# A first phase without lead pieces: reloads in another order, stores on ScalarE's queue, positions on SyncE's

## The chip, the cores and the metric

The kernel runs on one core of a Trainium2 chip. A core has five engines, each with its own instruction stream that it works through in order: TensorE (PE, matrix products), VectorE (DVE), ScalarE (ACT), GpSimd (POOL) and SyncE (SP, which computes nothing). SyncE, ScalarE and GpSimd also issue DMA transfers between the chip's memory (DRAM) and the core's on-chip memory; the core's 16 DMA engines carry them out. An instruction can wait for others by semaphores, and while it waits everything behind it on its engine waits too.

The metric is the time of one execution in device microseconds, lower is better. Most executions of one kernel agree within 0.3%.

## The reference

Two stages. The first convolves the product of x and v with a learned filter along the sequence, by Fourier transforms, and gates the result with x. The second sends about half of the rows through one of eight small expert networks. The change lies in the first stage.

```python
def _attn_ref(x, v, pos_emb, w1, w2):         # x, v: (4, 11456, 128)
    B, S, D = x.shape
    h_mlp = np.maximum(pos_emb @ w1, 0.0) @ w2     # pos_emb: (11456, 64)
    h_filt = h_mlp * np.exp(-0.01 * np.arange(S))[:, None]
    L = 2 * S
    Uf = np.fft.rfft(x * v, n=L, axis=1)
    Hf = np.fft.rfft(h_filt, n=L, axis=0)
    y = np.fft.irfft(Uf * Hf[None], n=L, axis=1)[:, :S]
    return x * y
...
    # then, row by row: if x @ w_skip > 0: out = x + gate * relu(x @ w1[e]) @ w2[e], else out = x
```

All of it is in float32.

## The kernel before

The sequence is cut into three blocks of 3840 = 60 x 64 rows, and the transform of one block is done in two steps: 60 points (k1) in a first phase, 64 points in a second, with the twiddle factors folded into the second one's matrices. The 128 channels are cut into four strips of 32. A *data step* is a sixteenth of a strip: it loads x and v (`wf<-xv`, 768 KB), multiplies them, transforms over 60 points (L202, two pieces of two products each), copies the result out of PSUM on ScalarE (L204) and stores it to DRAM (`x1d<-wf`, 720 KB). The strips have 64 steps in all, 0 to 15 for strip 0, and so on. The 64-point transform needs all steps of a strip, since it reads the stored rows in the other direction; that is why they go through DRAM.

**First phase** (`first_phase`, L276). It does the 16 data steps of strip 0 and, interleaved with them at a fixed pace, the filter (`First.filt`, L214): 12 position pieces (`post`, 256 KB each, L232, loaded from GpSimd's queue) go through w1 (L240, result `fa`) and relu (L241, `h`); then 24 groups go through w2 (L267), the window (L268, `hw`), the 60-point transform (L248) and a copy (L250, `fx`), and are stored to `x1f` in 16 transfers of 720 KB from GpSimd's queue (L256).

**Frequency phase** (`freq_phase`, L307). It runs 60 rounds, 15 for each strip. A round loads four k1 of a strip (`x<-x1d`, 768 KB, L362, and `x<-x1f`, 192 KB, L363; in strip 0 the matrix `c2` too, 256 KB, L359), three rounds ahead into four buffers; transforms them on PE (L373, `xp`); multiplies data and filter on VectorE (L385 to L393); adds on GpSimd (L465, L466); transforms back on PE (L404); copies on ScalarE (L405, `z`) and stores `zd` (L414). The data steps of the next strip are spread over the rounds of this one (`step`, L344): they must be done four rounds before the next strip begins. A round has one or two of them.

What sets the order around the change:

- Both phases are recorded in a fixed order, which is the order of the code on each engine. Between the phases an engine may take an instruction of the second early where nothing holds it (the first `c2` load is such a one).
- `First.ahead(step)` issues loads of x and v up to three steps ahead, into three buffers. In the first phase it runs at the first piece of each step, with `step + 1`.
- `First.mult` multiplies x and v, on VectorE in the first phase and on GpSimd in the frequency phase. There are two buffers for the products and four for the results.
- `First.data` keeps a step's store back in `late` until the first piece of the next step is done; `First.store` then issues it from SyncE (L190), where the loads of x and v stand as well.
- `LEAD = 6`: six pieces (the three steps 16, 17 and 18 of strip 1) are done ahead of the first frequency round, by the loop at L422, with their products on VectorE.

Of the kernel before, what the change touches and what calls it, by code (L numbers as in the profile page):

```python
# [22 lines left out]
K1, N2 = 60, 64  # L23
# [18 lines left out]
SOON = 4  # L42
NKNOWN = sum(n * u for c, n, u in KNOWN)
NEARLY = sum(n * u for c, n, u in KNOWN[:SOON])
LEAD = 6
FLEAD = 2
FEND = 2
KS = 4
QX = 4
# [94 lines left out]
class First:  # L144
# [22 lines left out]
        nc.sync.dma_start(self.c1, i["c1"])  # L167
        self.loaded, self.late = 0, []

    def ahead(self, step):  # L170

        while self.loaded < min(step + self.XV, self.ALL):
            self.load(self.loaded)
            self.loaded += 1

# [4 lines left out]
    def mult(self, step):  # L180
        if step < self.ALL:
            rows = slice(0, 64 + K1)
            xv = self.xv[step % self.XV][rows]
            eng = self.nc.vector if step < self.STEPS + LEAD // self.Q else self.nc.gpsimd
            eng.tensor_tensor(self.us[step % self.US][rows], xv[:, 0], xv[:, 1], ALU.mult)  # L185

    def store(self):

        for dst, xs in self.late:
            self.nc.sync.dma_start(dst, xs)  # L190
        self.late = []

    def data(self, step, pool):
# [4 lines left out]
        for q in range(Q):  # L198
            ps = [pool.tile([2 * K1, 512], F32, name="ps")[:, 0:RUN] for _ in range(2)]
            for p in range(2):  # L200
                rows = slice(p * 64, p * 64 + K1)
                nc.tensor.matmul(ps[p], self.c1[rows], u[rows, q * RUN:(q + 1) * RUN], start=True, stop=True)  # L202
            for p in range(2):
                nc.scalar.copy(xs[:, 2 * q + p], ps[p])  # L204
            if q == 0:
                self.store()
            if q < Q - 1:
                yield
        self.late.append((self.x1d[h][:, :, 2 * Q * ch:2 * Q * (ch + 1)].rearrange("k c m w -> (k c) m w"), xs))
        if ch == self.STEPS - 1:  # L210
            self.store()
        yield

    def filt(self, fc, fp, pool):  # L214
# [14 lines left out]
        def positions(blk, k):  # L229

            pt = fp.tile([128, P], F32, name="post", bufs=4)
            nc.gpsimd.dma_start(pt, i["post"][blk, k // P])  # L232
            return pt
        posts = [positions(*pc) for pc in pieces[:3]]
        yield
        for n, (blk, k) in enumerate(pieces):
            if n + 3 < len(pieces):
                posts.append(positions(*pieces[n + 3]))
            ps = pool.tile([128, P], F32, name="fa")
            nc.tensor.matmul(ps, w1, posts.pop(0), start=True, stop=True)  # L240
            nc.scalar.activation(hs[blk][:, k:k + P], ps, AF.Relu)  # L241
            yield

# [32 lines left out]
def first_phase(tc, fi):  # L276

    with (
# [6 lines left out]
        left = 0.0  # L285
        pieces = NB * 64 * H2 // 512 + 2 * NB * H2 // 4
        pace = (pieces - FLEAD) / (fi.Q * (fi.STEPS - FEND))
        next(f)
        fi.ahead(0)
        fi.mult(0)  # L290
# [16 lines left out]
def freq_phase(tc, nc, i, fi, zd, c3, spare, loads):  # L307
# [9 lines left out]
    with (  # L317
# [26 lines left out]
        def step():  # L344

            n = fi.STEPS * fi.Q
            credit[0] += (n - LEAD) / (PER - QX) if done[0] < n else n / PER
            while credit[0] >= fi.Q:
                credit[0] -= fi.Q
                for _ in range(fi.Q):  # L350
                    next(todo, None)

        def load(n):
# [5 lines left out]
                nc.sync.dma_start(c2(ks.start, KS), i["c2"][k])  # L359
            x1 = qx.tile([128, KS, (NS + NB) * DH], F32, name="x1")  # L360
            w = NB * DH
            nc.sync.dma_start(x1[:, :, 0:fi.RUN], fi.x1d[h][ks].rearrange("k c n w -> (c n) k w"))  # L362
            nc.sync.dma_start(x1[:, :, fi.RUN:], fi.x1f[ks, :, :, h * w:(h + 1) * w].rearrange("k c n w -> (c n) k w"))  # L363
            return x1

        def spread(n, j):
# [51 lines left out]
        done_z = []  # L418
        todo = others()
        ys = {}  # L420
        xs = {n: load(n) for n in range(QX - 1)}
        for _ in range(LEAD):  # L422
            next(todo)
        gs, xps = {}, {}

        def begin(n, j):
# [933 lines left out]
```

## Time and profile before

| what | value |
|---|---|
| time, median of 3 runs (lowest to highest) | 1628.69 us (1627.09 to 1629.76) |
| profiled execution, its own time | 1626.78 us |
| its span, from the first to the last instruction | 1625.0 us |
| PE busy | 1537.8 us (95%) |
| VectorE, ScalarE, GpSimd busy | 1203.4, 794.3, 1084.8 us |
| bytes read and written in DRAM | 216.96 and 145.69 MB |
| first phase, up to the first matmul of the frequency phase | 142.78 us |
| frequency phase, up to its last copies | to about 730 us |

The span in 40 slices of 40.6 us, with each digit a tenth (9 is 90% or more). `PEclk` is the clock granted to TensorE.

```profile
PE   7985999999999999996789999999989999999997
DVE  1324877888788799993877777777887777777886
ACT  4552455444544544442235544544345655556774
POOL 1112988888888878870156647855677888867885
PEclk9996999999999999997889999999999999999999
DMA  7998999999999799968978768877631111111110
```

The first three slices and half of the fourth are the first phase: the DMA engines are nearly full, VectorE and GpSimd are not. In the fourth slice PE drops to 5 tenths and its clock to 6. From the fifth slice on PE is at 9, with VectorE and GpSimd close behind.

How to read the views below: `SPq`, `ACTq` and `POOLq` are the instruction queues that issue transfers; `q` is left out where the engine computes. In a timeline a row gives start, duration, engine, line, operation, output and inputs, the number of instructions merged, and in brackets the idle time before and what ended it. A float32 matmul shows as two passes, so a data step (two pieces of two products) is 8 passes of L202.

### The profile page before, as it was taken

To read this page: it belongs to the slowest core of one execution; us is meant where nothing else is said; L and a number is where in the kernel's file an instruction comes from. 1 tells how busy PE (TensorE), PEld (TensorE's weight loads), DVE (VectorE), ACT (ScalarE), POOL (GpSimd) and SP (SyncE) were. 2 spreads that over 40 slices of the span, in tenths; PEclk is the share of its full clock that TensorE was granted. 3 is DMA by queue.
4 is the path that set the end of the run, shared out by engine and by line. 5 is a ranking of instruction groups with operands and counts; after the bars stand their busy time and mean duration, and the time that the engine had idled before them with its cause. 6 is when DMAs were issued, how large, how long until landed. Compare 5 with 4: busy or idle time off the path is not lost.

```text
span 1625.0 us, 26505 instructions
## 1 busy us (share of the span) xinstructions
PE 1537.8 (95%) x8272; PEld 961.0 (59%) x8272; DVE 1203.4 (74%) x2424; ACT 794.3 (49%) x1677; POOL 1084.8 (67%) x850
## 2 busy tenths in 40 slices
PE   7985999999999999996789999999989999999997
PEld 2552444444444444442347766666767888888997
DVE  1324877888788799993877777777887777777886
ACT  4552455444544544442235544544345655556774
POOL 1112988888888878870156647855677888867885
PEclk9996999999999999997889999999999999999999
DMA  7998999999999799968978768877631111111110
GB/s 283 333 339 315 379 377 377 356 329 335 321 343 338 255 265 316 312 160 295 301 222 255 229 214 257 255 223 240 209 87 33 47 45 47 45 37 37 38 36 23
DMA packets 198532, 361.92 MB, mean 223 GB/s; under 512 B 64650, under 2 KB 138778, under 8 KB 198350
## 3 DMA queue, kind: packets, MB, share of 16 engines
q1 hardware_dynamic: 181078, 320.12, 58.9%
q0 software_dynamic: 16704, 38.89, 8.5%
q8 instruction: 67, 1.10, 0.3%
q10 hardware_dynamic: 608, 1.20, 0.2%
q14 instruction: 75, 0.61, 0.1%
HBM read 216.96 MB, written 145.69 MB: 223 GB/s over the span
## 4 chain that ended last, share of the span: by engine, by line
PE 84%; DMA 6%; DVE 5%; issue 3%; POOL 1%; ACT 1%; SPq 0%; DVEq 0%; ACTq 0%; POOLq 0%
PE ps L404 20%; PE xp L373 12%; PE bank L782 6%; PE y L1018 5%; PE ps L202 5%; PE my L834 4%; PE my L832 4%; PE hp L700 4%; PE my L833 4%; PE hp L702 4%; PE hp L701 4%; PE mh L700 2%; PE tp L1031 2%; PE mh L702 1%; PE mh L701 1%
## 5 line engine op out<-in xcount | busy, mean ns | idle before, releaser
L404 PE MATMUL ps<-y,c 128*128 128x512 f32 x720 | 331.3, 597 | 0.3
L465 POOL TENSOR_TENSOR y<-y,p 128x2048 f32<-128x2048 f32 x59 | 267.7, 4537 | 68.8 <-DVE p L393 68.8
L706 POOL DMA_INDIRECT out<-o,ids x186 | 199.9, 1075 | 123.3 <-DVE o L713 87.0
L404 PEld LDWEIGHTS ps<-y,c 128*128 128x128 f32 x720 | 133.4, 190 | 173.0 <-issue 155.9
L637 POOL DMA_INDIRECT xt<-out,ids x186 | 193.1, 1038 | 49.3 <-issue 30.6
L393 DVE TENSOR_TENSOR p<-xp,g 128x1024 f32<-128x1024 f32 x240 | 217.4, 947 | 0.0
L393 DVE TENSOR_TENSOR y<-xp,g 128x1536 f32<-128x1536 f32 x120 | 210.8, 1757 | 4.1
L821 DVE SCALAR_TENSOR_TENSOR hh<-hp,hh 128x1024 fp32r<-128x1024 f32 x130 | 158.4, 1219 | 68.3 <-ACT hh L820 68.1
L405 ACT COPY z<-ps 128x512 f32<-128x512 f32 x180 | 105.6, 586 | 176.5 <-PE ps L404 167.5
L820 ACT ACTIVATE hh<-hp 128x1024 fp32r<-128x1024 f32 x130 | 134.2, 1032 | 75.4 <-PE hp L702 75.4
L589 POOL DMA_INDIRECT lists<-pl,lies x32 | 53.6, 1676 | 141.0 <-DVE step L1116 72.3
L466 POOL TENSOR_TENSOR y<-y,p 128x1024 f32<-128x1024 f32 x59 | 139.0, 2356 | 4.6
L677 DVE TENSOR_TENSOR ws<-wf,ws 128x1024 fp32r<-128x1024 f32 x104 | 126.7, 1219 | 15.5 <-ACT ws L672 12.1
L610 POOL MEMSET idle<- 128x512 f16 x248 | 134.6, 543 | 0.2
L1018 PE MATMUL y<-zt,c 128*64 128x512 f32 x384 | 114.1, 653 | 19.8 <-DMA zt<-zd 11.2
L700 PE MATMUL hp<-hl,ws 128*128 128x512 f32 (+1 forms) x344 | 123.3, 359 | 3.5 <-DVE tb L626 1.9
L202 PE MATMUL ps<-wf,c 60*120 60x384 f32 x512 | 111.8, 532 | 14.8 <-DVE wf L185 14.3
L782 PEld LDWEIGHTS bank<-wd,h 128*128 128x128 f32 x896 | 104.2, 191 | 31.5 <-issue 31.4
L373 PE MATMUL xp<-x,wf 128*128 128x480 f32 x256 | 115.5, 575 | 7.3 <-issue 3.6
L204 ACT COPY wf<-ps 120x384 f32<-120x384 f32 x256 | 105.5, 493 | 29.5 <-PE ps L202 28.9
L702 PE MATMUL hp<-hl,ws 128*128 128x512 f32 (+1 forms) x344 | 116.4, 338 | 0.0
L834 PE MATMUL my<-hh,ws 128*128 128x512 f32 (+1 forms) x344 | 116.3, 338 | 0.0
(162 smaller groups left out, 3062.1 us busy)
## 6 DMA issues: line engine op xcount, KB each, us to landing
wf<-xv SPq DMA_DIRECT2D x64, 768.0 KB
zt<-zd SPq DMA_DIRECT2D x64, 768.0 KB
x1d<-wf SPq DMA_DIRECT2D x64, 720.0 KB
x<-x1d SPq DMA_DIRECT2D x60, 768.0 KB
zd<-z SPq DMA_DIRECT2D x118, 384.0 KB
out<-xm SPq DMA_DIRECT2D x96, 258.0 KB
ox<-xo SPq DMA_DIRECT2D x96, 256.0 KB
x1f<-fx POOLq DMA_DIRECT2D x16, 720.0 KB
```

Source lines behind the costliest of these rows:

```text
L202: nc.tensor.matmul(ps[p], self.c1[rows], u[rows, q * RUN:(q + 1) * RUN], start=True, stop=True)
L373: nc.tensor.matmul(xp[:, k, 0:(NS + NB) * DH], c2(n % PER * KS + j * KH + k), x1[:, j * KH + k], start=True, stop=True)
L393: nc.vector.tensor_tensor(o[:, :, :, j * KH:(j + 1) * KH].rearrange("p s a k b d -> p (s a) k b d"), x[:, None].broadcast_to([128, m, KH, ...
L404: nc.tensor.matmul(zps, c3[:, a, :], y[:, blk, a], start=(a == 0), stop=(a == 1))
L465: nc.gpsimd.tensor_tensor(y[:, 1:], y[:, 1:], p1, ALU.add)
L637: ins = nc.gpsimd.indirect_dma_start(out=xt[:, j], out_offset=None, in_=self.rows[0:have], in_offset=bass.IndirectOffsetOnAxis(ap=ids[:, j ...
L700: nc.tensor.matmul(hp, w[:, 0, c], hl[:, 0], start=True, stop=False)
L702: nc.tensor.matmul(hp, w[:, 1, c], hl[:, 0], start=False, stop=True)
L706: ins = nc.gpsimd.indirect_dma_start(out=self.rows, out_offset=bass.IndirectOffsetOnAxis(ap=ids[:, j:j + 1], axis=0), in_=o, in_offset=Non ...
L782: nc.tensor.matmul(bank[:, j * D:(j + 1) * D], h[f][:, j * 128:(j + 1) * 128], wd[s][:, f * D:(f + 1) * D], start=(f == 0), stop=(f == F / ...
L834: nc.tensor.matmul(y, w2[:, 1, c], h[:, 0], start=False, stop=(f == F // 128 - 1))
L1018: nc.tensor.matmul(y[p * 64:(p + 1) * 64], c4s[ch // C4][:, ch % C4, p, :], z[:, NP * p:NP * (p + 1)], start=True, stop=True)
```

## The change

`LEAD` and its loop are gone; the products of steps from 16 on are GpSimd's. The stores of a step go out right behind its last copies, from ScalarE's queue. The positions are loaded from SyncE's queue, two ahead of the first x and v, two behind them, and then each behind the matmul that frees its buffer. In the frequency phase the reload asks for the filter's rows (`x1f`) ahead of the data's rows (`x1d`); for round 0 the data's rows come in four transfers, of which the last two hold the four rows that step 15 stores. `ahead` stops at the strip's end while it is called for a step of strip 0, and is called once more behind the reload of round 1.

```diff
-LEAD = 6
...
-    def ahead(self, step):
+    def ahead(self, step, most=XV):

-        while self.loaded < min(step + self.XV, self.ALL):
+        while self.loaded < min(step + most, self.ALL if step >= self.STEPS else self.STEPS):
             self.load(self.loaded)
             self.loaded += 1
...
-            eng = self.nc.vector if step < self.STEPS + LEAD // self.Q else self.nc.gpsimd
+            eng = self.nc.vector if step < self.STEPS else self.nc.gpsimd
...
         for dst, xs in self.late:
-            self.nc.sync.dma_start(dst, xs)
+            self.nc.scalar.dma_start(dst, xs)
         self.late = []
...
                 nc.scalar.copy(xs[:, 2 * q + p], ps[p])
-            if q == 0:
-                self.store()
             if q < Q - 1:
                 yield
         self.late.append((self.x1d[h][:, :, 2 * Q * ch:2 * Q * (ch + 1)].rearrange("k c m w -> (k c) m w"), xs))
-        if ch == self.STEPS - 1:
-            self.store()
+        self.store()
         yield
...
             pt = fp.tile([128, P], F32, name="post", bufs=4)
-            nc.gpsimd.dma_start(pt, i["post"][blk, k // P])
+            nc.sync.dma_start(pt, i["post"][blk, k // P])
             return pt
-        posts = [positions(*pc) for pc in pieces[:3]]
+        posts = [positions(*pc) for pc in pieces[:2]]
+        yield
+        posts += [positions(*pc) for pc in pieces[2:4]]
         yield
         for n, (blk, k) in enumerate(pieces):
-            if n + 3 < len(pieces):
-                posts.append(positions(*pieces[n + 3]))
             ps = pool.tile([128, P], F32, name="fa")
             nc.tensor.matmul(ps, w1, posts.pop(0), start=True, stop=True)
+            if n + 4 < len(pieces):
+                posts.append(positions(*pieces[n + 4]))
...
         next(f)
+        fi.ahead(0, 1)
+        next(f)
         fi.ahead(0)
...
             n = fi.STEPS * fi.Q
-            credit[0] += (n - LEAD) / (PER - QX) if done[0] < n else n / PER
+            credit[0] += n / (PER - QX) if done[0] < n else n / PER
...
             w = NB * DH
-            nc.sync.dma_start(x1[:, :, 0:fi.RUN], fi.x1d[h][ks].rearrange("k c n w -> (c n) k w"))
             nc.sync.dma_start(x1[:, :, fi.RUN:], fi.x1f[ks, :, :, h * w:(h + 1) * w].rearrange("k c n w -> (c n) k w"))
+            m = N2 - 2 * fi.Q
+            for lo, hi in ((0, m), (m, N2)) if n == 0 else ():
+                for c in range(2):
+                    nc.sync.dma_start(x1[c * N2 + lo:c * N2 + hi, :, 0:fi.RUN], fi.x1d[h][ks, c, lo:hi].rearrange("k n w -> n k w"))
+            if n:
+                nc.sync.dma_start(x1[:, :, 0:fi.RUN], fi.x1d[h][ks].rearrange("k c n w -> (c n) k w"))
...
-        xs = {n: load(n) for n in range(QX - 1)}
-        for _ in range(LEAD):
-            next(todo)
+        xs = {}
+        for n in range(QX - 1):
+            xs[n] = load(n)
+            if n == 1:
+                fi.ahead(fi.STEPS)
```

Three places in the built order. The first is the start of the first phase on SyncE and, for the stores, on ScalarE. Before, SyncE issues four loads of x and v (`wf<-xv`), and from then on a store (`x1d0<-wf`) stands ahead of each load:

```order
L223 DMA fw1_73<-w1 128x128
L178 DMA wf_58<-xv 128x1536 x4
L359 DMA wf_58<-c2 128x512
L190 DMA x1d0<-wf_58 120x1536
L178 DMA wf_58<-xv 128x1536
```

Now SyncE has positions and loads, and ScalarE the store, behind the copies (`wf<-ps`) of the step's second piece:

```order
L228 DMA post_82<-post 128x512
L228 DMA post_84<-post 128x512
L177 DMA wf_58<-xv 128x1536
L228 DMA post_87<-post 128x512
L228 DMA post_89<-post 128x512
L177 DMA wf_58<-xv 128x1536 x2
L228 DMA post_96<-post 128x512
L228 DMA post_101<-post 128x512
L177 DMA wf_58<-xv 128x1536
```

```order
L239 ACTIVATE h0_76<-fa_117 128x512
L203 COPY wf_58<-ps_122 120x384
L203 COPY wf_58<-ps_123 120x384
L189 DMA x1d0<-wf_58 120x1536
L239 ACTIVATE h1_77<-fa_129 128x512
```

The store left SyncE's queue and stands in ScalarE's stream, ahead of the next relu.

The second place is SyncE at the end of the first phase and the start of the frequency phase (`x1_850` is the buffer of round 0, `x1_854` or `x1_857` that of round 1). Before:

```order
L178 DMA wf_58<-xv 128x1536
L190 DMA x1d0<-wf_58 120x1536
L362 DMA x1_850<-x1d0 128x4x384
L363 DMA x1_850<-x1f 128x4x96
L359 DMA wf_58<-c2 128x512
L362 DMA x1_854<-x1d0 128x4x384
```

Now:

```order
L177 DMA wf_58<-xv 128x1536 x12
L362 DMA x1_850<-x1f 128x4x96
L366 DMA x1_850<-x1d0 60x4x384 x2
L366 DMA x1_850<-x1d0 4x4x384 x2
L359 DMA wf_58<-c2 128x512
L362 DMA x1_857<-x1f 128x4x96
L368 DMA x1_857<-x1d0 128x4x384
```

The twelve loads in a row are those of steps 7 to 18; the added call of `ahead` behind the reload of round 1 finds them issued and adds none. The filter's rows now come first, and the data's rows in four transfers.

The third place is PE in the third frequency round (`L202` is a data piece's matmul, `xp` the transform of a round, `ps<-y` the way back). Before:

```order
L404 MATMUL ps<-y,c_61 128x512 x4
L373 MATMUL xp_1046<-x_922,wf 128x480 x2
L202 MATMUL ps<-wf,c_59 120x384 x4
L404 MATMUL ps<-y,c_61 128x512 x2
L373 MATMUL xp_1078<-x_922,wf 128x480 x2
```

Now:

```order
L409 MATMUL ps<-y,c_61 128x512 x4
L378 MATMUL xp_1005<-x_880,wf 128x480 x2
L201 MATMUL ps<-wf,c_59 120x384 x8
L409 MATMUL ps<-y,c_61 128x512 x2
L378 MATMUL xp_1052<-x_880,wf 128x480 x2
```

This round has two data steps now instead of one. Of the first eleven rounds two had two data steps before, and five have two now. In exchange, the run of data matmuls right ahead of the first `xp` has become shorter, from 20 matmuls to 8: twelve matmuls (24 passes, three steps) left it.

## The prediction, made before the change was run

> **What bounds the kernel now.** I read the chain of work that ended last first, because the change touches one stage only and the chain says what that stage waits for. It prints start, duration, what.
>
> ```profile
> 17.23 8.31 DMA post<-post
> ...
> 118.83 18.50 DMA x1d<-wf
> 137.35 0.39 SPq L362
> ...
> 138.06 4.58 DMA x<-x1f
> ...
> 142.78 5.36 PE xp L373 x8
> ...
> 152.14 1.82 POOL wf L185
> ```
>
> The first phase ends with a transfer. The last store of strip 0 (x1d<-wf, L190) is issued at 118.83 and takes 18.50 us to land; only then does SyncE issue the first reload (L362, 137.35), and the first frequency matmul (L373) starts at 142.78. That instant, the **handover**, is what the change can move. The second view is the table of stretches: length, busy time of PE, PEld, DVE, ACT and POOL, granted clock, DMA share, GB/s.
>
> ```profile
> 0.00:3.00 3.00, 0.00 (x0) 0.00 (x0) 0.00 (x0) 0.00 (x0) 1.90 (x7) 1.00 0.38 94
> 3.00:30.00 27.00, 18.92 (x38) 6.15 (x40) 3.83 (x4) 10.63 (x19) 4.99 (x10) 0.88 0.97 362
> 30.00:35.00 5.00, 5.00 (x34) 2.45 (x32) 0.14 (x1) 2.98 (x7) 0.00 (x0) 0.95 0.04 18
> 35.00:45.00 10.00, 10.00 (x90) 6.27 (x90) 4.74 (x7) 5.80 (x12) 0.74 (x2) 1.00 0.87 241
> 45.00:130.00 85.00, 70.78 (x488) 40.85 (x484) 23.73 (x32) 42.49 (x92) 7.61 (x15) 0.92 0.96 339
> 130.00:137.50 7.50, 3.71 (x11) 1.75 (x13) 1.66 (x2) 1.72 (x4) 0.00 (x0) 0.50 0.43 159
> 155.00:260.00 105.00, 104.36 (x298) 45.52 (x295) 85.62 (x106) 53.78 (x141) 93.12 (x34) 1.00 1.02 379
> ```
>
> Up to the handover the DMA engines are the bound: share 0.96 at 339 GB/s from 45 to 130. They lose time in three places: they stand at 30 to 35 (share 0.04), run at 241 GB/s from 35 to 45, and thin out from 130 to 137.5 (159 GB/s). After the handover PE is the bound (104.36 of 105 us). So an us of waiting removed before 142.78 is an us won, and an us of PE work added after 155 is an us lost. Summed, the rows up to 137.5 carry 42.6 MB (94 x 3 + 362 x 27 + 18 x 5 + 241 x 10 + 339 x 85 + 159 x 7.5).
>
> **Why the DMA stood.** SyncE's queue in order of time:
>
> ```profile
> 23.28 0.33 SPq L178 DMA_DIRECT2D wf<-xv  x1
> 34.51 0.35 SPq L190 DMA_DIRECT2D x1d<-wf  x1
> 34.95 0.33 SPq L178 DMA_DIRECT2D wf<-xv  x1
> ```
>
> Its waits from 16 to 120 (us in total, times, longest), and VectorE's last product before that load:
>
> ```profile
> SPq L190 <- ACT wf L204: 80.2, 15, 10.9
> ```
>
> ```profile
> 21.99 0.96 DVE L185 TENSOR_TENSOR wf<-wf 124x768 f32<-124x768 f32 x1 [5.08 <-PE ps L202]
> ```
>
> The load at 34.95 needed a buffer that VectorE had finished reading at 22.95 (21.99 + 0.96), but it stood behind a store that waited for ScalarE's copies until 34.51. Stores waited 80.2 us in all for copies, each time with the next load behind them. These copies were late because positions came late (8.31 us in the chain). In the built order of the changed kernel no load in this stage has a store ahead of it on SyncE.
>
> **The change part by part.**
>
> *1. Stores on ScalarE's queue, positions on SyncE's.* Loads now wait only for their own buffers and for position rows, and the stores go out behind the copies that they need. I count the stretch at 30 to 35 as filled: 5 x (339 - 18) / 339 = 4.7 us. The stretch at 35 to 45 likewise, since up to three loads are then outstanding: 10 x (339 - 241) / 339 = 2.9 us. For 130 to 137.5, which would be 7.5 x (339 - 159) / 339 = 4.0 us, I take nothing: the last stores still have to finish on whichever DMA engine is last. Bounds: 0 (the bytes queue up again later) to 11.6 us (all three filled). Value taken: 7.6 us.
>
> The Trainium skill speaks against this part: "DMA: Bandwidth & Descriptors", section "Issuing engines are not separate DMA queues", says that DMAs from all issuing engines run on the same 16 engines, and that spreading them saves only the issuing time. By that rule this term is 0, not 7.6. The stretch at share 0.04 shows what the rule does not speak of: a load not yet issued because of what stands ahead of it. Whether the engines are then fuller overall, no run here shows yet.
>
> *2. The first reload.* Before, two transfers of 768 and 192 KB wait for the last store: 142.78 - 137.35 = 5.4 us. Now the 192 KB of x1f go first, 60 of 64 rows of x1d wait for the stores up to the second last, and two pieces of 24 KB each wait for the last one. The trace has no piece this small ahead of a waiting matmul. Its price lies between the two issues alone (0.39 each, 0.8 us) and the present 5.4. The sizes:
>
> ```profile
> wf<-xv SPq DMA_DIRECT2D x64, 768.0 KB
> x<-x1d SPq DMA_DIRECT2D x60, 768.0 KB
> x<-x1f SPq DMA_DIRECT2D x60, 192.0 KB
> ```
>
> I take 3.4, because the large part is still in flight when the last store lands: 2.0 us won, bounds 0 and 4.6. What the few words promise, rows ahead of later x and v, holds only from step 19 on: the built order still has the loads of steps 16 to 18 (3 x 768 KB, 2.36 MB, 7.0 us at 339 GB/s) ahead of the first reload, because the last call of the first phase asks for them. I give nothing for those.
>
> *3. The lead pieces.* Three data steps (24 passes of L202) leave the stretch before the handover, where they cost nothing:
>
> ```profile
> 121.55 2.92 PE L202 MATMUL ps<-wf,c 60*120 60x384 f32 x8 [5.00 <-DVE wf L185]
> 130.85 2.92 PE L202 MATMUL ps<-wf,c 60*120 60x384 f32 x8 [6.38 <-DVE wf L185]
> 136.71 2.92 PE L202 MATMUL ps<-wf,c 60*120 60x384 f32 x8 [2.94 <-DVE wf L185]
> ```
>
> They run beside the 18.50 us wait. Now they are in the first eleven frequency rounds, where PE is full: five rounds with two data steps instead of two. The price is the difference between a round with one and a round with two:
>
> ```profile
> 190.22 1.61 PE xp L373 x4
> ...
> 200.32 1.61 PE xp L373 x4
> 201.93 1.48 PE ps L202 x8
> 203.41 0.01 issue
> 203.42 1.96 PE ps L202 x7
> ...
> 212.34 1.61 PE xp L373 x4
> ```
>
> One round is 200.32 - 190.22 = 10.10, the next 212.34 - 200.32 = 12.02. Three times 1.92 is **5.8 us lost**. It is nearly certain, since the chain there is PE without a gap. GpSimd takes three more products. Its row from 155 to 260:
>
> ```profile
> L185 POOL TENSOR_TENSOR wf<-wf 124x768 f32<-124x768 f32 x13 | 23.7, 1821 | 6.9 <-DVE g L386 6.9
> ```
>
> Of its 93.12 us there, 23.7 are products, so some 69.4 are ten rounds of additions, 6.9 each; 11 x 6.9 + 16 x 1.82 = 105 us, under PE's 6 x 10.10 + 5 x 12.02 = 120.7. DMA: the same bytes are left after the handover as before it (loads from step 19, stores from step 16), and there is a little more time for them, so nothing is added.
>
> *4. Handover.* Two rows of PE, from its timeline and from the chain:
>
> ```profile
> 151.69 1.85 PE L373 MATMUL xp<-x,wf 128*128 128x480 f32 x4 [3.56 <-issue]
> ```
>
> ```profile
> 154.01 1.60 PE ps L202 x8
> ```
>
> PE waited from 153.5 to 154.0 for the product at 152.14, that of step 19; that product now belongs to a step whose rows are there earlier: 0.5 us won, bounds 0 and 0.5.
>
> *5. Stores in ScalarE's instruction stream.* This is the added wait. Behind each store stand the copies of z (L405) and g (L376 to L378), for which PE and VectorE wait. Rows for its price are the issues (ns, min/median/max), SyncE's waits from 150 to 300, ScalarE's z copies from 155 to 260, and its copies in a round with two data steps:
>
> ```profile
> L190 SPq DMA_DIRECT2D x1d<-wf x64: 317/388/2376, 16.8 to 565.3; - x64
> ```
>
> ```profile
> SPq L363 <- DMA x<-x1d: 11.3, 7, 1.8
> ```
>
> ```profile
> L405 ACT COPY z<-ps 128x512 f32<-128x512 f32 x29 | 17.0, 586 | 29.3 <-PE ps L404 29.3
> ```
>
> ```profile
> 202.80 3.16 ACT L204 COPY wf<-ps 120x384 f32<-120x384 f32 x8
> ```
>
> An issue is 0.39 us in the median; ScalarE idles 29.3 / 29 = 1.0 us ahead of each z copy, and is busy 53.78 of 105. So an issue alone is covered. What may exceed the cover is a wait for an earlier transfer, as SyncE shows at L363 (11.3 / 7 = 1.6 us, 1.8 at most), since each transfer in the built program also waits for one some eight before it. It hurts most between two data steps of one round, where ScalarE has eight copies in a row (3.16 us). Bounds: 0, and 16 stores x (1.6 + 0.4 - 1.0) = 16 us. I take 0.5, near the covered issue.
>
> **Sum** against the profiled execution (1626.78 us, of which the span is 1625.0 and 1.8 lie around it): -7.6 - 2.0 + 5.8 - 0.5 + 0.5 = -3.8, which gives 1623.0. That execution is 1.9 under the median of the three runs (1628.69), from which the same sum gives 1624.9. I predict **1624**.
>
> **Rivals.**
>
> *A, the tail fills as well.* The last store has a queue without loads ahead of it. For it: 18.50 us for 720 KB is mostly queueing. The Trainium skill (same page, "Queues, rings and completion order") says that an engine takes turns between the queue rows it has work for. That favours the store; the trace of before, with loads and stores on one queue, can't show it. Against: x1f stores and three loads share the same engines. It adds up to the 4.0 us left out and 2 more of the reload: -3.8 - 6 = -10, about 1617 to 1619.
>
> *B, the bytes decide, not the gap.* If the transfers won at 30 to 45 only wait later, term 1 is 0: -2.0 + 5.8 - 0.5 + 0.5 = +3.8, about 1630.6 to 1632.5, on the edge between no difference and slower. For it: share 0.96 for 85 us. Against: engines that stood for 5 us moved nothing then, and nothing later gives those 5 us back unless the end had room. The rule named in part 1 gives the same.
>
> *C, slower: ScalarE is held by its stores.* In each of the five double rounds the second store waits for a transfer issued in the same round. If that wait passes the 1.0 us of cover by 1.6 us in each, and in half of the other six, PE loses 8 x 1.6 = 13 us: -3.8 + 13 = +9, about 1637. It decides from a total of 4 us on; below that the forecast's sign holds.
>
> **How the numbers follow.** Forecast (-7 to -1) 0.48; A 0.17; B 0.21; C 0.14. A difference of 0.2%, 3.3 us, is about what a measurement of this kernel can tell from no change, so faster means under 1625.4: all of A and some 0.38 of the forecast's 0.48, together 0.55. Slower means over 1632: most of C and a little of B, 0.15. The rest, 0.30, is within. The range takes the forecast, A, and B with the weak half of C: 1616 to 1632.
>
> **What would show it.** Term 1: in the stretch from 25 to 45 the DMA share stays over 0.9 and positions are waited for less than 8 us. Handover: the first L378 matmul near 133 rather than 142.78; its wait ends with a small x1d piece, not with x1f. Term 3: five rounds of about 12.0 us among the first eleven. Term 5: ScalarE's idle time ahead of z copies released by DMA stays under 1 us in sum. I am wrong if the handover comes after 138 (B), or if frequency rounds are longer than 10.1 and 12.0 us with PE waiting for ScalarE's g or z copies (C).

## The result, and the profile after

| | before | after |
|---|---|---|
| time, median of 6 runs each (lowest to highest) | 1627.89 us (1626.45 to 1630.32) | 1645.05 us (1642.61 to 1650.16) |
| profiled execution, and its span | 1626.78, 1625.0 | 1645.12, 1643.3 |
| handover (first frequency matmul) | 142.78 | 142.20 |
| from the handover to round 12 | 121.8 | 137.9 |

The change makes the kernel slower: the ratio is 1.0108, 95% interval 1.0093 to 1.0123. I had forecast 1624, with a range of 1616 to 1632. One of the seven runs of s1 below took 2479.54 us at a granted clock of 0.568 (the others 1632.24 to 1640.13), and its ratio is taken without that run.

First the chain of waits of the changed kernel up to the handover (start, duration, what):

```profile
86.71 18.02 DMA x1f<-fx
...
124.81 9.25 DMA x1d<-wf
...
134.16 0.79 SPq L366
...
135.47 5.95 DMA x<-x1d
...
142.20 6.24 PE xp L378 x8
```

The last store goes out 6 us later than before (124.81 against 118.83) but lands in half the time, at 134.06. From there to the first matmul pass 8.1 us, where it was 5.4. The same stretches as before the change (length, busy time of PE, PEld, DVE, ACT, POOL, granted clock, DMA share, GB/s):

```profile
30.00:35.00 5.00, 5.00 (x50) 3.29 (x52) 2.25 (x3) 2.60 (x6) 0.00 (x0) 1.00 0.98 387
35.00:45.00 10.00, 10.00 (x90) 6.30 (x88) 3.22 (x5) 6.60 (x14) 1.30 (x2) 1.00 0.88 265
45.00:130.00 85.00, 68.31 (x456) 39.00 (x452) 21.51 (x29) 39.42 (x84) 10.82 (x16) 0.86 0.92 321
130.00:137.50 7.50, 0.00 (x0) 0.00 (x0) 0.00 (x0) 0.00 (x0) 0.00 (x0) 0.50 0.70 222
155.00:260.00 105.00, 98.64 (x278) 43.38 (x276) 72.70 (x90) 49.97 (x131) 84.92 (x32) 0.97 0.95 327
```

The gap at 30 to 35 us is filled, as forecast (share 0.98 after 0.04). But from 45 to 130 us the rate is 321 GB/s where it was 339: 1.5 MB less in those 85 us, nearly as much as the early gap had won (5 us x (387 - 18) GB/s = 1.8 MB). And after 155 us PE, which had been full, idles 6.4 us of 105. ScalarE's waits for transfers, first up to 143 us, then from 143 to 320 us (us in total, times, longest):

```profile
ACT fx L248 <- DMA x1f<-fx: 18.5, 6, 5.8
```

```profile
ACT z L410 <- DMA wf<-xv: 14.6, 4, 4.0
PE ps L409 <- ACT wf L203: 6.2, 3, 2.9
...
ACT wf L203 <- DMA c<-c: 5.2, 2, 3.3
ACT z L410 <- DMA x<-x1f: 4.2, 1, 4.2
...
ACT wf L203 <- DMA wf<-c: 2.3, 1, 2.3
```

The first row was 11.9 us before the change. The second block was all but absent: a z copy waited 1.1 us for a transfer. What such a wait is can be seen in ScalarE's timeline of a round with two data steps:

```profile
198.16 0.32 ACTq L189 DMA_DIRECT2D x1d<-wf  x1
198.52 1.63 ACT L203 COPY wf<-ps 120x384 f32<-120x384 f32 x4 [2.33 <-DMA wf<-c]
203.82 0.32 ACTq L189 DMA_DIRECT2D x1d<-wf  x1
204.19 0.58 ACT L410 COPY z<-ps 128x512 f32<-128x512 f32 x1 [4.04 <-DMA wf<-xv]
```

The copies of the second data step end at 200.15, but its store is issued only at 203.82. It does not wait for its own data: the idle time ends with the landing of a load of x and v. The z copy at 204.19 needs nothing of that load; it stands behind the store. SyncE had issued the load in this same round:

```profile
192.32 3.39 SPq L177 DMA_DIRECT2D wf<-xv  x2
```

Of these two loads the first went out at 192.32. In the trace it has the store's completion semaphore and stands eight issues ahead of it, counted over SyncE's and ScalarE's queues together; the store goes out as it lands, 11.5 us after its issue. On PE:

```profile
191.92 1.77 PE L378 MATMUL xp<-x,wf 128*128 128x480 f32 x4
193.62 3.53 PE L201 MATMUL ps<-wf,c 60*120 60x384 f32 x16
199.06 3.63 PE L409 MATMUL ps<-y,c 128*128 128x512 f32 x4 [1.90 <-ACT wf L203]
202.52 1.77 PE L378 MATMUL xp<-x,wf 128*128 128x480 f32 x4
...
207.56 1.77 PE L378 MATMUL xp<-x,wf 128*128 128x480 f32 x4
```

That round takes 207.56 - 191.92 = 15.6 us, not 12.0. By the starts of the rounds in this timeline the double rounds take 12.1, 15.6, 13.5, 16.7 and 12.1 us; the single rounds between them take 10.1 us, as before.

So there are two questions: why did the handover not move, and what do the stores cost in the frequency rounds?

### The profile page after: what moved, and what is told of

Read it like the earlier page. It is cut to its first block, busy times and chain, and to the rows that moved or that the text cites. A ratio compares the mean times of both kernels' runs of the same rounds, so it can differ in the third digit from the quotient of the medians.

```text
span 1643.3 us, 26480 instructions
## 1 busy us (share of the span) xinstructions
PE 1543.5 (94%) x8272; PEld 963.9 (59%) x8272; DVE 1201.4 (73%) x2421; ACT 795.8 (48%) x1677; POOL 1083.9 (66%) x841
## 4 chain that ended last, share of the span: by engine, by line
PE 80%; DMA 10%; DVE 6%; issue 2%; ACT 1%; SPq 0%; POOL 0%; ACTq 0%; DVEq 0%; POOLq 0%
PE ps L409 18%; PE xp L378 11%; PE bank L789 5%; PE y L1025 5%; PE ps L201 4%; PE my L841 4%; PE my L839 4%; PE hp L707 4%; PE my L840 4%; PE hp L709 4%; PE hp L708 4%; DMA zd<-z 3%; DMA x1f<-fx 2%; PE mh L707 2%; PE tp L1038 2%
## 5 line engine op out<-in xcount | busy, mean ns | idle before, releaser
L684 DVE TENSOR_TENSOR ws<-wf,ws 128x1024 fp32r<-128x1024 f32 x104 | 126.8, 1219 | 15.5 <-ACT ws L679 13.3
L378 PE MATMUL xp<-x,wf 128*128 128x480 f32 x256 | 118.0, 586 | 21.2 <-DMA x<-x1d 18.5
L390 DVE TENSOR_TENSOR g<-xp,g 128x128 f32<-128x128 f32 x120 | 34.8, 290 | 126.0 <-ACT g L383 121.7
L789 PEld LDWEIGHTS bank<-wd,h 128*128 128x128 f32 x896 | 104.2, 191 | 31.5 <-issue 31.4
L841 PE MATMUL my<-hh,ws 128*128 128x512 f32 (+1 forms) x344 | 116.3, 338 | 0.0
L839 PE MATMUL my<-hh,ws 128*128 128x512 f32 (+1 forms) x344 | 116.3, 338 | 0.0
```

Source lines behind the costliest of these rows:

```text
L378: nc.tensor.matmul(xp[:, k, 0:(NS + NB) * DH], c2(n % PER * KS + j * KH + k), x1[:, j * KH + k], start=True, stop=True)
L789: nc.tensor.matmul(bank[:, j * D:(j + 1) * D], h[f][:, j * 128:(j + 1) * 128], wd[s][:, f * D:(f + 1) * D], start=(f == 0), stop=(f == F / ...
L839: nc.tensor.matmul(y, w2[:, 0, c], h[:, 0], start=(f == 0), stop=False)
L841: nc.tensor.matmul(y, w2[:, 1, c], h[:, 0], start=False, stop=(f == F // 128 - 1))
```

## Experiments

Ratios are to the kernel before on the same chip, with 95% intervals. Each kernel has one profile, from which the handover is read. The changed kernel and s1 have the same first phase, and their handovers are 142.2 and 143.0, so a difference of an us is not read as an effect. The second group ran on a chip on which the kernel before took 1651.6 us, so of its times only the ratios count, and its handovers stand beside those of other chips with that reserve.

### First group: the parts put back

*s1*: the changed kernel, stores from strip 1 on back on SyncE.

```diff
+            if q == 0:
+                self.store(nc.sync)
...
-        self.store()
+        if h == 0:
+            self.store()
+        elif ch == self.STEPS - 1:
+            self.store(nc.sync)
```

> The changed kernel, but from strip 1 of the first transform on (its data steps that run inside the frequency rounds) the stores of x1d leave from SyncE again, one pass behind their copies as before the change. Theory H (ScalarE is held at its stores in the double rounds, and PE waits for the g and z copies behind them): the 2nd to 4th double round fall from 15.6, 13.5 and 16.7 us to about 12.1, the waits of ScalarE's z copies that end with a DMA fall from about 19 us in sum to under 3, and the time falls by 9 to 11 us, to about 1635; five double rounds remain, so some 6 us over the kernel before stay. Rival R (the DMA engines are too full in the first eleven rounds, whoever issues): the long rounds stay, with the waits now at SyncE or at xp, and the time stays within 3 us of 1645.

Measured: 1636.77 us (median of seven), ratio 1.0046 (1.0029 to 1.0063). No wait of ScalarE from 143 to 320 us ends with a transfer but 3.4 us in all for z's own buffer. The round that had taken 15.6 us, on PE:

```profile
192.13 1.77 PE L383 MATMUL xp<-x,wf 128*128 128x480 f32 x4
193.83 3.52 PE L201 MATMUL ps<-wf,c 60*120 60x384 f32 x16
197.29 1.98 PE L414 MATMUL ps<-y,c 128*128 128x512 f32 x4
199.11 1.77 PE L383 MATMUL xp<-x,wf 128*128 128x480 f32 x4
...
204.15 1.77 PE L383 MATMUL xp<-x,wf 128*128 128x480 f32 x4
```

204.15 - 192.13 = 12.0 us. From handover to round 12 it takes 127.8 us: of the 16.1 us by which the changed kernel was longer there, 10.1 belong to ScalarE's late stores, and 6.0 are left for the lead pieces. Theory H holds; rival R falls, since the same bytes move and no round is long.

*s2*: the changed kernel with `LEAD = 6` and its lines back, the stores still all on ScalarE's queue.

> The changed kernel with the six lead pieces (three data steps) back ahead of the first frequency matmul, the stores all on ScalarE's queue. Theory H: two double rounds instead of five among the first eleven, so 3 x 1.9 = 5.8 us of PE work leaves, and of the 9.7 us of stalls only those of at most two double rounds are left: time 1629 to 1634. Rival R: with three data steps earlier the transfers have less to do in the rounds, but the handover comes later, as those steps' loads share the DMA engines with the reload: 1637 to 1642.

Measured: 1637.63 us, 1.0050 (1.0033 to 1.0067). There are two double rounds of 12.1 us, without a stall, as theory H has it; but its time of 1629 to 1634 was missed. The time and the later handover are rival R's: the second round takes 11.6 us instead of 8.0, and the handover is at 148.0. In this profile the early gap was half open again (share 0.63 from 30 to 35 us, against 0.98 in s3, whose code up to there is the same), so it may be a late one. Why stays open.

*s3*: both put back, so that only the first phase differs from the kernel before. *s4*: the same with four fx buffers.

```diff
-            xs = [fp.tile([2 * K1, M, NP, NB, DH], F32, name=f"fx{p}") for p in range(2)]
+            xs = [fp.tile([2 * K1, M, NP, NB, DH], F32, name=f"fx{p}", bufs=4) for p in range(2)]
```

> Lead pieces back, and the stores from strip 1 on back on SyncE: against the kernel before only the first phase is changed (its stores on ScalarE's queue, positions on SyncE's, the split first reload). Theory H: frequency rounds as before, and only the handover moves, by what it moved in the changed kernel (0.6 us): 1625 to 1630, no difference from before that can be measured. Rival R, in the form that the handover was held back only by what the change does behind it: a handover at 133 to 138 and 1618 to 1624.

> As the kernel with lead pieces and late stores put back, but with four buffers instead of two for the rows of fx that the stores of x1f read. Theory F (the gain at 30 to 45 us is given back between 45 and 130 us because the x1f stores, alone on GpSimd's queue, take 18 us each beside two other queues, and ScalarE's fx copies wait 18.5 us in sum for their two buffers): those waits go, the stretch from 45 to 130 us rises from 321 towards 339 GB/s, and the handover comes 3 to 6 us earlier, so the time is 3 to 6 us under the two-buffer one. Rival G (the DMA engines' rate with three queues of mixed sizes is itself lower): the fx waits go, but the rate stays near 321 GB/s and the handover moves by under 1 us.

Measured: s3 1631.97 us, 1.0017 (1.0001 to 1.0033), handover 144.5, rounds as before the change; the time is 2 us over theory H's range, and the handover moved the other way. So what the change does to the first phase wins nothing by itself. s4: 1628.88 us, 1.0002 (0.9988 to 1.0016), handover 140.8. The stretches of s3 and of s4:

```profile
45.00:90.00 45.00, 39.73 (x288) 23.02 (x286) 13.35 (x18) 21.59 (x46) 4.14 (x8) 0.89 0.89 297
```

```profile
45.00:90.00 45.00, 45.00 (x378) 27.11 (x376) 16.95 (x23) 29.23 (x64) 5.18 (x10) 1.00 0.98 349
90.00:130.00 40.00, 19.27 (x102) 9.76 (x100) 6.68 (x8) 14.25 (x33) 2.07 (x4) 0.71 0.82 307
```

With four buffers ScalarE's fx waits fall from 15.8 to 0.6 us and the rate from 45 to 90 us rises from 297 to 349 GB/s, as theory F has it. But the loss now sits at the end. SyncE's queue waits there for the x1f stores (100 to 160 us):

```profile
SPq L368 <- DMA x1f<-fx: 34.4, 4, 28.4
```

GpSimd had issued the last of them by 100.2 us; they landed at 132.8. The queues of s4 (q0 is GpSimd's, q10 ScalarE's, q1 SyncE's: packets, MB, share of the 16 engines), from 80 to 90 and from 120 to 125 us:

```profile
q0 software_dynamic: 238, 1.19, 34.9%
q10 hardware_dynamic: 213, 1.17, 31.4%
q1 hardware_dynamic: 228, 1.24, 31.0%
...
q0 software_dynamic: 180, 0.96, 51.8%
q10 hardware_dynamic: 25, 0.13, 8.0%
```

While all three have work, each gets about a third; the x1f stores fall behind and are left over when the others are done.

### Second group: is it the queue?

*b1*: the kernel before with four fx buffers. *s5*: the changed kernel with late stores on SyncE, four fx buffers, and the loads of steps 16 to 18 really behind the first reloads. *s6*: s4 with the x1f stores on ScalarE's queue. *s7*: s4 with the first reload whole.

```diff
s5
-                    fi.ahead(step + 1)
+                    fi.ahead(min(step + 1, fi.STEPS - 1))
s6
-                nc.gpsimd.dma_start(self.x1f[:, :, n0:n0 + M]...
+                nc.scalar.dma_start(self.x1f[:, :, n0:n0 + M]...
s7
+            nc.sync.dma_start(x1[:, :, 0:fi.RUN], fi.x1d[h][ks].rearrange("k c n w -> (c n) k w"))
             nc.sync.dma_start(x1[:, :, fi.RUN:], fi.x1f[ks, :, :, h * w:(h + 1) * w].rearrange("k c n w -> (c n) k w"))
-            m = N2 - 2 * fi.Q
-            for lo, hi in ((0, m), (m, N2)) if n == 0 else ():
...
```

> The kernel before, with four buffers instead of two for the rows of fx. Theory F (two buffers are too few only because the changed kernel's stores of x1f share the DMA engines with two other queues): before, ScalarE's fx copies wait 11.9 us for their buffers, the stretch from 45 to 90 us already runs at 337 GB/s, and the handover moves by under 1.5 us from 142.8. Rival (two buffers cost the same in both kernels, so the gain of four says nothing of the change): the handover comes 3 to 4 us earlier, near 139.

> The changed kernel with its late stores on SyncE and four fx buffers, no lead pieces, and the loads of steps 16 to 18 held back until two reloads are issued (what the change's few words say; in the changed kernel they are issued ahead of the first reload). Theory B (until the handover the bytes decide: those three loads are 2.36 MB, 7 us of all DMA engines): the handover comes at 132 to 136 instead of 140.8, with 5.8 us to pay for five double rounds: time 1621 to 1626. Rival (the tail behind the last load decides: product, matmul, copy, store, reload, one behind the other): the handover stays at 138 to 141, and the time is 1628 to 1632.

> The kernel with lead pieces, late stores on SyncE and four fx buffers, but the stores of x1f leave from ScalarE's queue too, right behind the copies that they need. Theory Q (each of the three queues that have work gets a third of the DMA engines' time, so the queue with the x1f stores, 34% of the time and issued by 100 us, drains last, at 132.8 us, and the first reload waits for it): with two queues the loads get half, the data steps run earlier, and the last x1f store no longer outlasts the x1d stores; the handover comes 2 to 6 us before 140.8. Rival H2 (ScalarE is held again, now in the first phase, because its stores wait for transfers some eight issues earlier): ScalarE's fx and data copies wait for DMAs by 20 us or more in sum, and the handover comes after 143.

> The kernel with lead pieces, late stores on SyncE and four fx buffers, but the first reload in two transfers as before the change: the whole of x1d, then x1f. Theory S (the split with x1f first costs time: five issues of 0.4 us each, and rows of x1f that wait for the slowest queue): from the moment at which the stores have landed, the first matmul follows after 5.4 us, as before the change, and not after the 8.0 us (132.8 to 140.8) of the split form: the handover comes 1.5 to 3 us earlier, at 138 to 139.5. Rival (the small pieces help, as I predicted, by 2 us): the handover is 1 to 3 us later.

| | ratio | handover | GB/s 45 to 90 us |
|---|---|---|---|
| b1 | 0.9986 (0.9963 to 1.0009) | 147.1 | 334 |
| s5 | 1.0006 (0.9979 to 1.0033) | 137.3 | 348 |
| s6 | 0.9907 (0.9875 to 0.9939) | 129.8 | 371 |
| s7 | 0.9997 (0.9964 to 1.0030) | 138.5 | 345 |

b1: the buffers alone change nothing in the kernel before; its handover came later than either theory had it. The handover of s5 lies between those of its two theories: without those 2.36 MB the first reload still waits 41.2 us for x1f stores. s6 is the answer. With one queue for both kinds of stores the handover comes 11 us earlier than in s4, on another chip, and 8.7 us earlier than in s7, on the same one (with the first reload whole); both are more than theory Q's 2 to 6 us. Its picture of halves was wrong, though. The queues of s6 from 60 to 70 us:

```profile
q10 hardware_dynamic: 422, 2.29, 65.8%
q1 hardware_dynamic: 233, 1.28, 31.3%
```

The loads (q1) have about what they had, and what was a third each for two queues of stores is now one queue's. Rival H2 falls: ScalarE's data and fx copies wait 10.2 us in sum for transfers, not 20. s7 came earlier than the split form, as theory S had it, but that comparison is between two chips; s9 below repeats it. s7 also shows what a last part costs by itself. Its x1d rows were issued at 129.83, and only its x1f rows, 192 KB, still waited for stores; they were issued at 135.70, and PE followed 2.8 us later:

```profile
138.47 5.13 PE L379 MATMUL xp<-x,wf 128*128 128x480 f32 x8 [11.80 <-DMA x<-x1f]
```

### Third group: what is enough

*a1*: the changed kernel with s6's edit alone. *s8*: s6 with two fx buffers. *s9*: s6 with the first reload whole. *p1*: s6 with positions on GpSimd's queue.

> The changed kernel with one edit: the stores of x1f leave from ScalarE's queue instead of GpSimd's. Theory Q (the x1f stores, alone on the third queue, get a third of the DMA engines' time and drain last; that is what took back the gain at 30 to 45 us): the handover comes 8 to 12 us before the changed kernel's 142.2, at 130 to 134, though fx has two buffers only; the stalls of the double rounds stay, so the time is 1 to 8 us above the kernel before. Rival F2 (four fx buffers are what freed the first phase, and the queue matters only on top of them): the handover stays at 139 to 142, and the time 14 to 18 us above the kernel before.

> Lead pieces back, late stores back on SyncE, x1f stores on ScalarE's queue, and two fx buffers as in both given kernels. Theory Q: a handover at 130 to 134, rounds as before the change, and a time 8 to 12 us under the kernel before (ratio 0.993 to 0.995). Rival F2: a handover at 139 to 143, and no difference from before.

> Lead pieces back, late stores on SyncE, x1f stores on ScalarE's queue, four fx buffers, and the first reload whole, x1d ahead of x1f as before the change. Theory S (the split first reload costs 2 to 3 us: five issues, of which two wait one behind the other; with the split form 9.4 us passed from 120.4, the first issue, to the first matmul at 129.8): the handover comes 2 to 4 us earlier than with the split, at 126 to 128, and the time is 10 to 16 us under the kernel before. Rival (the split helps once the x1f stores are not the last): the handover is at 130 to 133.

> Lead pieces back, late stores on SyncE, x1f stores on ScalarE's queue, four fx buffers, the split first reload, but the position rows from GpSimd's queue, as before the change. If the stores that left SyncE's queue alone fill the early gap (my term 1 as I argued it): the DMA share from 30 to 35 stays over 0.9 and the handover is within 1 us of 129.8. If the positions' move is what fills it: the share from 30 to 35 falls under 0.5, and the handover comes 2 to 5 us later.

| | median us | ratio | handover | to round 12 |
|---|---|---|---|---|
| a1 | 1630.38 | 1.0012 (1.0000 to 1.0024) | 134.4 | 133.3 |
| s8 | 1615.45 | 0.9914 (0.9883 to 0.9944) | 132.7 | 123.1 |
| s9 | 1613.64 | 0.9913 (0.9896 to 0.9931) | 131.2 | 122.4 |
| p1 | 1620.08 | 0.9945 (0.9923 to 0.9967) | 131.7 | 123.4 |

In a1 that one edit moves the handover from 142.2 to 134.4, with two fx buffers. From its chain of waits:

```profile
71.26 14.37 DMA x1f<-fx
...
118.83 9.74 DMA x1d<-wf
128.58 5.14 DMA x<-x1d
134.40 4.88 PE xp L378 x8
```

The x1f store in this chain takes 14.4 us; the two in the changed kernel's took 17.7 and 18.0 (by the landings in the traces all sixteen take 5.3 to 18.2 us there, and 6.1 to 15.3 in a1). The last x1d store goes out at 118.83, 6 us earlier than in the changed kernel. Theory Q holds, with a handover just outside its 130 to 134; rival F2 falls. The double rounds of a1 cost less than those of the changed kernel: 133.3 us to round 12, which is 5.5 over s1 where the changed kernel is 10.1 over it. s8 and s9 run some 14 us under the kernel before (1629.15 here) by their ratios: these two beat both given kernels, as s6 does and, by less, p1. Theory Q had 8 to 12 us for s8. The handover makes 10.1 us of it, and 11.6 in s9; where the rest comes from is not shown. The DMA rate of s8 from 45 to 90 us is 364 GB/s.

s9 does not show what theory S asked for: 131.2 lies in the range of the rival, between s6 (129.8) and s8 (132.7). Its rows say why. SyncE, then PE:

```profile
125.81 0.39 SPq L368 DMA_DIRECT2D x<-x1d  x1
```

```profile
131.23 6.11 PE L379 MATMUL xp<-x,wf 128*128 128x480 f32 x8 [9.47 <-DMA x<-x1f]
```

The whole reload takes 131.23 - 125.81 = 5.4 us from its issue, as before the change. In a1, split, it is 134.40 - 128.57 = 5.8 us from the landing of the last store. So the small pieces neither won nor cost much; but in a1 they went out at 128.58, right behind the large ones, of which the first was issued at 126.75. In the changed kernel x1f stores held all of the reload until 133.59, where its first transfer was issued, with the other four behind it up to 136.1:

```profile
133.59 0.39 SPq L362 DMA_DIRECT2D x<-x1f  x1
```

p1 looks at the early gap:

```profile
30.00:35.00 5.00, 5.00 (x36) 2.48 (x34) 0.20 (x1) 2.92 (x6) 0.00 (x0) 0.94 0.11 47
```

With positions back on GpSimd's queue the gap is open again (share 0.11), no store standing ahead of any load; and the handover is at 131.7 all the same, between s6 (129.8) and s8 (132.7), where the gap is closed. That is the second outcome that I had written down, at its edge: it comes 2.0 us after s6, on another chip, where I had 2 to 5. Its ratio lies 0.3% above those of s8 and s9, from a single round of timing.

### Fourth group: single edits to the kernel before

*b2*: x1f stores on ScalarE's queue. *b3*: the first phase's x1d stores on ScalarE's queue. *b4*: positions on SyncE's, in the order of the changed kernel.

```diff
b2
-                nc.gpsimd.dma_start(self.x1f[:, :, n0:n0 + M]...
+                nc.scalar.dma_start(self.x1f[:, :, n0:n0 + M]...
b3
-        if ch == self.STEPS - 1:
+        if h == 0:
+            self.store(nc.scalar)
+        elif ch == self.STEPS - 1:
             self.store()
b4
-            nc.gpsimd.dma_start(pt, i["post"][blk, k // P])
+            nc.sync.dma_start(pt, i["post"][blk, k // P])
...
```

> The kernel before with one edit: the stores of x1f leave from ScalarE's queue instead of GpSimd's; positions stay on GpSimd's queue, stores of x1d on SyncE's. Theory Q3 (what counts is that loads, x1d stores and x1f stores lie on no more than two queues and that x1f is not the last; before, with x1d stores and loads in one queue, x1f had its half and was not the last): nothing to win, handover 141 to 144, time within 0.3% of the kernel before. Rival E (the x1f stores are simply better on ScalarE's queue, whatever else is changed): handover 131 to 136, time 6 to 11 us under the kernel before.

> The kernel before with one edit: the first phase's stores of x1d leave from ScalarE's queue right behind their copies; later stores, positions, lead pieces and the first reload as before. Theory Q (three queues with work, the x1f stores drain last): the x1f stores take 15 to 18 us each, the handover stays at 141 to 145 and the time within 0.3% of the kernel before, although no load stands behind a store on SyncE. Rival (my term 1 as predicted: the early gap closes, since no load stands behind a store): the DMA share from 30 to 35 us is over 0.9 and the handover at 134 to 138.

> The kernel before with one edit: positions from SyncE's queue, in the order of the changed kernel; stores and lead pieces as before. If late positions made the early gap (the run with positions back on GpSimd's queue had a DMA share of 0.11 at 30 to 35 us): the share there is over 0.7, and, as the bytes behind it decide, the handover comes only 0 to 3 us before 142.8. Rival (a load behind a waiting store made it): the gap stays, with a share under 0.3, and the handover moves by under 1 us or comes later.

| | ratio | handover | share 30 to 35 us | GB/s 45 to 90 us |
|---|---|---|---|---|
| b2 | 1.0011 (0.9995 to 1.0028) | 143.9 | 0.18 | 334 |
| b3 | 1.0001 (0.9988 to 1.0015) | 141.6 | 0.53 | 299 |
| b4 | 1.0021 (1.0009 to 1.0032) | 143.1 | 0.50 | 332 |

None wins anything by itself. In b2, the waits of SyncE's queue up to 145 us; in b3, a wait of ScalarE in the same time:

```profile
SPq L190 <- ACT wf L204: 76.1, 15, 10.2
```

```profile
ACT fx L252 <- DMA x1f<-fx: 17.8, 6, 5.8
```

In b2 loads still stand behind x1d stores that wait for copies, so the loads come late. In b3 they do not, but now three queues have work, and ScalarE stands for its fx buffers. With both kinds of store off SyncE's and GpSimd's queues (a1, s6, s8, s9, p1) the handover moves by 8 to 13 us; in every other kernel it comes at most 5.5 us earlier than before (s5).

## Why the prediction was wrong, step by step

**Term 1 (stores on ScalarE's queue, positions on SyncE's: -7.6 us) failed.** The stretch at 30 to 35 us did fill, yet the handover moved by 0.6 us, and in s3, with the lead pieces in place, it came 1.7 us later than before. The step that failed leads from the filled stretch to the time: "I count the stretch at 30 to 35 as filled: 5 x (339 - 18) / 339 = 4.7 us." My rival B said that the bytes only wait later, and that is what happened; but the reason is not the bytes either. s8, s9 and p1 move the same ones to a handover at 131 to 133. With the x1d stores on ScalarE's queue three queues had work, and the x1f stores lay alone on one of them: the two in the chain took 17.7 and 18.0 us, where the one in the chain of before took 15.0, ScalarE stood 18.5 us for their two buffers, where it had stood 11.9, and the first reload waited for the last of them until 133.59. a1 shows that it is the queue of the x1f stores that held the handover (one edit, 7.8 us earlier). b3, with nothing moved but the x1d stores, has the same waits, and in s4, without those waits, the x1f stores still land last. Whether the number of queues slows them or GpSimd's queue itself stays open.

Of the early gap I had named both causes, loads behind stores and late positions, but no run weighs them. Taking the stores off SyncE (b3) and moving the positions (b4) each raised the share there to about 0.5, both together to 0.98; but p1 has 0.11 with its stores off SyncE as in b3. It does show that the gap can be there with no store ahead of any load. Against s6 it puts the worth of closing it at some 2 us of handover, by one profile each.

The rule that I had set against this term, from the Trainium skill ("DMA: Bandwidth & Descriptors", section "Issuing engines are not separate DMA queues"), gives 0 for it, and 0 is what was measured. But its reason, that a move between issuing engines saves only the issuing time, does not carry through these runs: a1 differs from the changed kernel by the issuing engine of 16 stores alone, and is 8 us earlier at the handover. The section "Queues, rings and completion order" of the same page, that a DMA engine takes turns between the rows it has work for, agrees with the three shares of s4 (34.9, 31.4 and 31.0%), but not with the two of s6 (65.8 and 31.3%), if turns are to mean equal shares of time: by the trace at least one load was under way on SyncE's queue all through those 10 us. I had used it in rival A for the last x1d store, which did land sooner (9.25 us after 18.50); I did not apply it to the x1f stores.

**Term 2 (first reload: -2.0 us) failed.** I took 3.4 us from the last store's landing to the matmul, on the ground that the large part would be on its way by then. It was not: with the x1f rows first, and held by x1f stores until 133.59, all five transfers were issued within 2.5 us, and 8.1 us passed, not 5.4. In a1, where the large pieces were issued up to 1.8 us ahead of the small ones, it was 5.8. So the price of a small piece by itself is not shown. s7 comes nearest, with the large part issued 5.9 us ahead: its last 192 KB took 2.8 us, less than my 3.4.

**Term 3 (lead pieces: +5.8 us) was right.** s1 has five rounds of 12.0 to 12.3 us and 127.8 us to round 12, 6.0 more than before.

**Term 4 (-0.5 us)** did not come: the second round takes 8.6 us, and took 8.0.

**Term 5 (ScalarE's stores: +0.5 us) was mis-sized.** The mechanism was that of rival C, above all the second store of a double round waiting for a transfer of the same round, and the bounds (0 to 16) held it; it cost 10.1 us, nearly all of it in three of the five double rounds. I had judged it by SyncE's waits of 1.6 us at L363. Here the wait is for what is left of a load that takes 11.5 us from its issue to its landing, and z copies stood up to 4.0 us for it. "Near the covered issue" was the wrong end to choose. The size is no constant: the same stores cost 5.5 us in a1, and the two double rounds of s2 have no stall.

**Sum.** Handover -0.6, lead pieces with the second round +6.0, late stores +10.1 make 15.5 us at round 12 (280.1 against 264.6), and 15.4 us are left at the end of the frequency rounds. Of the 22.1 us between my sum (-3.8) and the span's growth (18.3), the handover makes 9.0 and the late stores 9.6. Rivals B and C came true together, for which I had no sum. The last 2.9 us arise in the output phase, which the change does not touch; over the other kernels of the same chip speed that remainder lies anywhere from -3.5 to +3.4 us, so I put it down to scatter, without proof.

## What to carry to other kernels

Before counting an idle gap of the DMA engines as time won, ask which transfer lands last at the barrier behind it, and which queue that one shares; a queue that is relieved may only put another one last, and four edits that each win nothing (b1 to b4) won some 14 us together (s9). A store put in the instruction stream of a computing engine makes that engine wait for whatever the store's issue waits for, which may be an unrelated transfer that another engine issued shortly before: price it at what may be left of that transfer's flight, not at the issue. Cutting a last dependent reload into pieces promises something only if the large ones are under way before the last wait ends, and here they were not: look first for what holds the queue that issues them.

## What I had not expected of the hardware

With both kinds of store on one queue the DMA engines moved 363 to 371 GB/s from 45 to 90 us (a1, s6, s8, s9, p1), against 345 to 349 with x1f stores on GpSimd's queue and four fx buffers (s4, s5, s7). No run separates whether GpSimd's queue itself costs that, or the third queue. b2 speaks against the first, without settling it: there the x1f stores leave GpSimd's queue alone, and the rate stays at 334 GB/s, where it was 337; but in b2 loads still wait behind stores. On one chip the kernel before took 1651.6 us (1642.7 to 1658.71) where it took 1628 to 1629 on the others.
